# First batch of a talking-heads attention kernel: logits of 19 chunks from weighted q, without a relayout

## The chip, the cores and the metric

The kernel runs on one core of a Trainium2 chip. The metric is the time on the device in microseconds (us), as the median of three runs; lower is better. The engines are PE (TensorE, matrix products), DVE (VectorE), ACT (ScalarE), POOL (GpSimd) and SP (SyncE, which here only issues DMAs); PEld is the loading of weights into PE.

## What is computed

Attention of 12 heads whose logits are mixed over the heads before the softmax and whose weights are mixed again after it ("talking heads"), followed by a feed-forward layer with a squared relu. There are 8 batches of 448 positions, a head has 64 elements, the model 768, the hidden layer 2048.

```python
def _attn_ref(q, k, v, w_pre, w_post):
    scale = 1.0 / np.sqrt(q.shape[-1])
    scores = scale * np.matmul(q, k.transpose(0, 1, 3, 2))
    scores = np.einsum('bhij,hg->bgij', scores, w_pre)
    scores = scores - np.max(scores, axis=-1, keepdims=True)
    attn = np.exp(scores)
    attn = attn / (np.sum(attn, axis=-1, keepdims=True) + 1e-09)
    attn = np.einsum('bhij,hg->bgij', attn, w_post)
    return np.matmul(attn, v)

def _moe_ref(x, w_in, w_out):        # x: attention, heads side by side
    h = np.maximum(x @ w_in, 0.0)
    return h * h @ w_out
```

## The kernel before

A batch has 448 query rows: 384 in three blocks (r = 1, 2, 3) of 128, and a tail of 64 (r = 0). Heads go in six pairs: kt holds, for a pair, the transposed keys with one head on partitions 0 to 63 and the other on 64 to 127, qz the transposed queries of the three blocks, zt those of the tail, with zeros for the head that isn't meant.

*Scores (L660).* For each head of a block one matmul with 64 partitions and 448 columns (two heads of a pair run side by side on PE's halves), for the tail one matmul per pair. DVE or ACT copies each from PSUM to a store snat (L426, L428), whose partitions are query rows.

*Relayout (L689).* The mixing needs heads on partitions. SP issues DMAs that move 10 rows of all 12 heads (120 partitions, a chunk) from snat to a buffer sch. A batch has 45 chunks: 6 of the tail, 13 each of the blocks. Chunk 0 of a block (positions C0[1] = 6, C0[2] = 19, C0[3] = 32 of the list) takes what is left over: the last 8 rows of the block and rows of the tail or of the next block; C0[2] has its own buffer schl.

*Mixing (L784).* One matmul with the weights wmix (w_pre spread over the 10 rows, times the negative scale) makes a chunk's 120 x 448 logits. In the first batch the tail's and the first block's chunks go in threes instead: one DMA of 315 KB moves three chunks to a buffer tri (in osb or h2, which are free then), and a chunk takes three matmuls with weights wtri (L780), which are made at the start on DVE, PE and ACT (L460, L465, L472, L480, L482).

*Then, for each chunk:* minimum over a row on DVE (L789; logits have the sign turned), exponential with its sum on ACT (L792), reciprocal on DVE (L798), the second mixing's weights times that reciprocal on POOL (wq, L801), four matmuls that mix and transpose (L808), and a copy to atb by DVE or ACT. AV (L848) runs when the chunks of a block are there, its result goes to xt by ACT (L858). The feed-forward layer goes in units of 128 or 256 rows: L901 (first product), relu on ACT (L914), square on POOL (L917), L933 (second product), a copy to osb on DVE (L948), stores by SP.

*What sets the order.* A planner in the kernel itself (class Planner) simulates the engines with the costs given in `add` and writes each engine's instructions out in the order that it finds; the chip then waits where data is late. An operation has a priority, mostly its chunk's place n in the list, less some distance: a relayout has n - AHEAD, scores a little less. The feed-forward matmuls have a priority far behind all others and fill what PE has left over. Where PE would be idle early on, the planner puts in matmuls on zeros (still, L1144), which keep PE's clock up. The costs and due times near the change are these:

```python
AHEAD = 7.4
LOADS0 = [("k", 0), ("t", 0), ("t", 1), ("k", 1), ("k", 2), ("q", 0), ("q", 1), ("q", 2)]
ORDER0 = [
    *range(EARLY), *[C0[1] + 1 + c for c in TRIPLES], C0[1], *range(EARLY, C0[1]),
    C0[2], *[C0[2] + 1 + c for c in TRIPLES], C0[3], *[C0[3] + 1 + c for c in TRIPLES],
]
...
        m = m_op[n] = add(
            "PE", 570 if three else 190, n, keep(mk, f_m),
            relay[n] + [at_op.get(n - NE)] + (tri_ready[sub(b, c)] if three else [w_ready]), lat=200, bank=mk,
        )
```

At the start POOL issues the loads of k, q and the tail of q (L348, L354, L359), then, behind a small copy that waits for the tail's scores (hold, L1067), those of v and of w_in (w1, L1019). SP first issues two small DMAs that repeat w_pre and w_post over the partitions (L380, L381).

Of the kernel before, what the change touches and what calls it, by code (L numbers as in the profile page):

```python
# [11 lines left out]
F32 = mybir.dt.float32  # L12
# [30 lines left out]
AHEAD = 7.4  # L43
# [11 lines left out]
LOADS0 = [("k", 0), ("t", 0), ("t", 1), ("k", 1), ("k", 2), ("q", 0), ("q", 1), ("q", 2)]  # L55
# [3 lines left out]
def spans(odd, half):  # L59
# [8 lines left out]
TRIPLES = [4 * m + t for t in range(4) for m in range(3)]  # L68
EARLY = 6
ORDER0 = [  # L70
    *range(EARLY), *[C0[1] + 1 + c for c in TRIPLES], C0[1], *range(EARLY, C0[1]),
    C0[2], *[C0[2] + 1 + c for c in TRIPLES], C0[3], *[C0[3] + 1 + c for c in TRIPLES],
]
NTRI = 5
SOON = 0
TRI_IN = (0, 1)
W2_AT = [18, 21, 24, 27]
Q1_AT = [13, 16]
LAST_W1 = 4
TAIL0, Q0 = 19, 0.7  # L80
EARLY0 = 0
# [36 lines left out]
class Planner:  # L118
# [18 lines left out]
    def run(self):  # L137
# [39 lines left out]
        while True:  # L177
            for eng, heap in ready.items():
# [53 lines left out]
                if item is None and eng == "PE" and free and IDLE_FROM <= t < IDLE_END and (  # L232
                    clock.at(t) > 1 or clock.share(t - SPELL, t) < IDLE_LOW
# [66 lines left out]
def kernel(  # L300
# [66 lines left out]
    nc.vector.memset(qt[:, :, :], 0.0)  # L367
    for what in LOADS0:
        if what[0] == "k":
            load_kv(ks, k, 0, 4 * what[1], 4 * what[1] + 4)  # L370
        elif what[0] == "q":
            load_q(0, 4 * what[1], 4 * what[1] + 4)
        else:
            load_tail(0, what[1])
        if what == LOADS0[0]:
            masks.make_identity(nc, ident[:, :])
# [22 lines left out]
    for t_ in wmix[1:]:  # L399
# [10 lines left out]
    keep_m = sb.tile([KC, 3], F32, name="keep_m")  # L410
    nc.vector.tensor_reduce(
        out=keep_m[:, :], in_=ident[0:KC, 0:KC].rearrange("p (s m g) -> p m s g", s=CI, m=3), axis=AX.XY, op=ALU.add,
    )
    pick = [h2[0][0:KC, f, 0:KC] for f in range(6)]
    wtri_all = sb.tile([KC, 18, P], BF16, name="wtri_all")
    wtri = [[wtri_all[:, 3 * m + x, :] for x in range(3)] for m in range(6)]
    nc.gpsimd.memset(wtri_all[:, :, KC:P], 0.0)
    tri = [t_[0:KC, 0:3 * S // 2].bitcast(BF16).rearrange("k (x s) -> k x s", x=3) for t_ in osb]
    tri += [
        h2[1][0:KC, :, :].rearrange("k f c -> k (f c)")[:, 3 * S * i:3 * S * (i + 1)].rearrange("k (x s) -> k x s", x=3)  # L420
        for i in range(3)
# [32 lines left out]
    set_up = add("DVE", 6300, -100, lambda: None)  # L454

    def pick_one(tail, x):
        to = pick[3 * tail + x]
        if tail:
            for m in range(3):
                nc.vector.tensor_copy(  # L460
                    out=to[:, :].rearrange("k (s m x g) -> k m s x g", s=CI, m=3, x=2)[:, m],
                    in_=ident[0:KC, 0:KC].rearrange("k (s g y x) -> k y s x g", s=CI, g=2, y=3)[:, x],
                )
        else:
            nc.vector.tensor_copy(  # L465
                out=to[:, :].rearrange("k (s m g) -> k s m g", s=CI, m=3),
                in_=ident[0:KC, 0:KC].rearrange("k (s g x) -> k x s g", s=CI, x=3)[:, x].unsqueeze(2).to_broadcast([KC, CI, 3, 4]),
            )

    def spread(tail, slot):  # L470
        for x in range(3):
            nc.tensor.matmul(  # L472
                slot[0:KC, x * KC:(x + 1) * KC], lhsT=pick[3 * tail + x][:, :], rhs=wmix[1][:, 0:KC], start=True, stop=True,
            )

    def thin(eng, tail, m):
        src = slots["g", "tri", tail][0:KC, 0:3 * KC].rearrange("p (x k) -> p x k", x=3)
        to = wtri_all[:, 9 * tail + 3 * m:9 * tail + 3 * m + 3, 0:KC]
        if eng == "DVE":
            nc.vector.tensor_scalar(out=to, in0=src, scalar1=keep_m[:, m:m + 1], scalar2=1.0, op0=ALU.mult, op1=ALU.mult)  # L480
        else:
            nc.scalar.activation(out=to, in_=src, func=ACT.Copy, scale=keep_m[:, m:m + 1])  # L482

    tri_ready = {}
    for tail in (1, 0):
        key = ("g", "tri", tail)
        at_pri = -30 if tail else -17
        picks = [add("DVE", 250, at_pri, lambda tail=tail, x=x: pick_one(tail, x), [set_up]) for x in range(3)]
        mm = add("PE", 200, at_pri, keep(key, lambda slot, tail=tail: spread(tail, slot)), picks, lat=200, bank=key)
        thins = []  # L490
        for m in range(3):
            thins.append(add(
                {"DVE": 500, "ACT": 560}, 0, at_pri + 0.1 * m, lambda eng, tail=tail, m=m: thin(eng, tail, m), [mm],
            ))
            tri_ready.setdefault(3 * tail + m, []).append(thins[-1])
        free_ = add("FREE", 0, at_pri, lambda: None, thins, lat=0, frees=key)
# [9 lines left out]
    def used(b, piece):  # L506
        i = 2 * b + piece - NSLOT
        return [score_ops[i // 2, NJ, PIECE * (i % 2) + x] for x in range(PIECE)] if i >= 0 else []
# [34 lines left out]
    def t_tail(b, g):  # L543
        key = ("f" if b == 0 else "g", "z", b, g)
        old = [score_ops[b - 1, 0, p] for p in range(3 * g, 3 * g + 3)] if b > 0 else []
# [12 lines left out]
        pri = b * NCHUNK - (19 if b > 0 else TAIL0) + 3 * g  # L558
# [3 lines left out]
        for p in range(3 * g, 3 * g + 3):  # L562
            ready_tail[b, p] = ev

# [620 lines left out]
```

## Time and profile before

| | us |
|---|---|
| median of three runs | 589.08 (588.86 to 589.49) |
| the profiled execution | 587.99 |
| its span in the trace | 586.2 |
| PE busy | 569.0 (97%) |
| of that, matmuls on zeros (L1144), 51 | 8.9 |
| DVE / ACT / POOL busy | 486.9 / 470.5 / 326.4 |
| first mixing matmul (L780) | starts at 18.94 |
| first feed-forward matmul (L901) | starts at 54.17 |

Busy time of PE is modelled with the end of each matmul, so one that stands alone looks longer than its place in a row of them: the distance of two starts is the price. The granted clock is PE's, 1.00 being full. A group's row gives its line, engine, operation, output and inputs, count, busy us, mean ns of one, and the idle time of the engine just before, with what ended it.

The largest groups of the chunks' work:

```profile
L792 ACT ACTIVATE es<-bank,mn 120x448 bf16<-120x448 f32 x360 | 229.6, 644 | 39.2 <-DVE mn L789 34.1
L789 DVE TENSOR_REDUCE mn<-bank 120x1 f32<-120x448 f32 x360 | 210.2, 612 | 7.7 <-PE bank L780 4.5
L426 DVE CAST snat<-bank 128x448 bf16<-128x448 f32 x164 | 96.3, 614 | 4.8 <-PE bank L660 3.3
L428 ACT CAST snat<-bank 128x448 bf16<-128x448 f32 x172 | 84.9, 551 | 3.7 <-PE bank L660 2.9
L801 POOL TENSOR_SCALAR wq<-wback,rc 120x120 bf16<-120x120 f32 x360 | 130.6, 367 | 179.1 <-DVE rc L798 104.0
```

### The profile page before, as it was taken

To read this page: it belongs to the slowest core of one execution; us is meant where nothing else is said; L and a number is where in the kernel's file an instruction comes from. 1 tells how busy PE (TensorE), PEld (TensorE's weight loads), DVE (VectorE), ACT (ScalarE), POOL (GpSimd) and SP (SyncE) were. 2 spreads that over 40 slices of the span, in tenths; PEclk is the share of its full clock that TensorE was granted. 3 is DMA by queue.
4 is the path that set the end of the run, shared out by engine and by line. 5 is a ranking of instruction groups with operands and counts; after the bars stand their busy time and mean duration, and the time that the engine had idled before them with its cause. 6 is when DMAs were issued, how large, how long until landed. Compare 5 with 4: busy or idle time off the path is not lost.

```text
span 586.2 us, 17120 instructions
## 1 busy us (share of the span) xinstructions
PE 569.0 (97%) x5802; PEld 407.8 (70%) x5802; DVE 486.9 (83%) x1241; ACT 470.5 (80%) x1239; POOL 326.4 (56%) x600
## 2 busy tenths in 40 slices
PE   8798999999999999999999999999999999999996
PEld 5446866777668676767767776876767766868783
DVE  5698999998899999999898888989798898989201
ACT  4597998889888898988888878888889888788330
POOL 4537557546666538744865538744856633735340
PEclk9899999999999999999999999999999999999999
DMA  8999969964796449965797639954597547322021
GB/s 96 190 216 221 208 143 174 192 160 116 130 196 164 122 115 173 190 134 142 114 173 171 135 100 173 184 146 124 100 176 177 133 112 146 102 82 79 1 55 54
DMA packets 132086, 82.33 MB, mean 140 GB/s; under 512 B 59582, under 2 KB 126286, under 8 KB 131998
## 3 DMA queue, kind: packets, MB, share of 16 engines
q1 hardware_dynamic: 85214, 58.42, 41.1%
q0 software_dynamic: 46784, 22.81, 30.9%
q8 instruction: 45, 0.74, 0.6%
q14 instruction: 43, 0.35, 0.2%
HBM read 45.62 MB, written 11.01 MB: 97 GB/s over the span
## 4 chain that ended last, share of the span: by engine, by line
PE 85%; ACT 4%; DMA 3%; DVE 3%; POOL 2%; issue 2%; SPq 0%; DVEq 0%; POOLq 0%; ACTq 0%
PE bank L933 24%; PE bank L901 24%; PE bank L808 13%; PE bank L784 10%; PE bank L848 6%; PE bank L660 6%; ACT es L792 2%; DMA sch<-snat 1%; DVE mn L789 1%; DMA osb<-snat 1%; PE bank L780 1%; ACT snat L428 1%; ACT hr L914 1%; PE bank L522 1%; DMA qt<-in_q_dram 1%
## 5 line engine op out<-in xcount | busy, mean ns | idle before, releaser
L792 ACT ACTIVATE es<-bank,mn 120x448 bf16<-120x448 f32 x360 | 229.6, 644 | 39.2 <-DVE mn L789 34.1
L801 POOL TENSOR_SCALAR wq<-wback,rc 120x120 bf16<-120x120 f32 x360 | 130.6, 367 | 179.1 <-DVE rc L798 104.0
L789 DVE TENSOR_REDUCE mn<-bank 120x1 f32<-120x448 f32 x360 | 210.2, 612 | 7.7 <-PE bank L780 4.5
L933 PE MATMUL bank<-w,h 128*128 128x384 bf16 x896 | 174.3, 325 | 0.9 <-ACT es L792 0.5
L426 DVE CAST atb<-bank 112x480 bf16<-112x480 f32 (+3 forms) x227 | 142.5, 636 | 28.9 <-PE bank L808 26.2
L901 PE MATMUL bank<-xt,w 128*128 128x256 bf16 (+1 forms) x1632 | 164.5, 253 | 0.2
L901 PEld LDWEIGHTS <-w 128*128 128x128 bf16 x1632 | 135.7, 98 | 21.9 <-issue 2.3
L917 POOL TENSOR_TENSOR h<-hr 128x512 bf16<-128x512 f32 x112 | 116.3, 1039 | 54.2 <-ACT hr L914 51.9
L808 PEld LDWEIGHTS <-es 120*112 120x112 bf16 (+1 forms) x1440 | 116.7, 130 | 38.2 <-issue 7.6
L808 PE MATMUL bank<-wq,es 120*112 120x120 bf16 (+1 forms) x1440 | 129.1, 217 | 3.0 <-POOL wq L801 2.0
L933 PEld LDWEIGHTS <-h 128*128 128x128 bf16 x896 | 83.5, 97 | 54.9 <-issue 5.2
L784 PE MATMUL bank<-sch,wmix 120*128 120x448 bf16 x334 | 103.2, 353 | 0.3
L426 DVE CAST snat<-bank 128x448 bf16<-128x448 f32 x164 | 96.3, 614 | 4.8 <-PE bank L660 3.3
L428 ACT CAST atb<-bank 112x480 bf16<-112x480 f32 (+3 forms) x157 | 82.5, 541 | 16.3 <-PE bank L808 14.7
L914 ACT ACTIVATE hr<-bank 128x512 f32<-128x512 f32 x112 | 67.1, 599 | 30.9 <-PE bank L901 25.2
L428 ACT CAST snat<-bank 128x448 bf16<-128x448 f32 x172 | 84.9, 551 | 3.7 <-PE bank L660 2.9
L792 ACT ACTIVATION_READ_ACCUMULATOR es<-bank,mn 120x1 f32 x360 | 76.0, 211 | 0.0
L798 DVE RECIPROCAL rc<-sm 120x1 f32<-120x1 f32 x360 | 53.4, 155 | 14.2 <-ACT es L792 12.0
L948 DVE COPY osb<-bank 128x384 f32<-128x384 f32 x56 | 30.9, 551 | 31.6 <-PE bank L933 31.3
L660 PE MATMUL bank<-kt,qz 64*128 64x448 bf16 x288 | 42.5, 354 | 0.4 <-ACT atb L428 0.2
L784 PEld LDWEIGHTS <-wmix 120*128 120x128 bf16 x342 | 30.3, 98 | 16.6 <-issue 6.7
L848 PE MATMUL bank<-atb,vs 112*64 112x192 bf16 (+3 forms) x864 | 41.0, 250 | 0.4 <-ACT atb L428 0.4
(60 smaller groups left out, 261.8 us busy)
## 6 DMA issues: line engine op xcount, KB each, us to landing
sch<-snat SPq DMA_DIRECT2D x318, 105.0 KB
out_dram<-osb SPq DMA_DIRECT2D x23, 360.0 KB
vs<-in_v_dram POOLq DMA_DIRECT2D x16, 336.0 KB, 9.0
ks<-in_k_dram POOLq DMA_DIRECT2D x14, 336.0 KB, 9.9
qs<-in_q_dram POOLq DMA_DIRECT2D x14, 288.0 KB, 8.9
w<-in_moe_w_in_dram POOLq DMA_DIRECT2D x6, 512.0 KB, 20.9
w<-in_moe_w_out_dram POOLq DMA_DIRECT2D x4, 768.0 KB, 25.1
out_dram<-osb SPq DMA_DIRECT2D x8, 192.0 KB
```

Of the source, the lines that this page charges most:

```text
L426: nc.vector.tensor_copy(out=out_, in_=in_)
L428: nc.scalar.copy(out=out_, in_=in_)
L660: nc.tensor.matmul(slot[:, 0:S], lhsT=lhsT, rhs=kt[i][half, :, at_, :], start=True, stop=True)
L784: nc.tensor.matmul(slot[:, 0:S], lhsT=wm[0:rows, :], rhs=src[0:rows, :], start=True, stop=True,)
L789: nc.vector.tensor_reduce(out=mn[i][0:rows, :], in_=slots[mk][0:rows, 0:S], axis=AX.X, op=ALU.min)
L792: nc.scalar.activation(out=es[i][0:rows, 0:S], in_=slots[mk][0:rows, 0:S], func=ACT.Exp, scale=-1.0, bias=mn[i][0:rows, 0:1], accum_out=sm ...
L801: nc.gpsimd.tensor_scalar(out=wq[i][0:rows, :, 0:ns], in0=wback[0:rows, :, 0:ns], scalar1=rc[i][0:rows, 0:1], scalar2=1.0, op0=ALU.mult, o ...
L808: nc.tensor.matmul(slot[0:P_KEYS, jb * H * ns:(jb + 1) * H * ns], lhsT=es[i][0:rows, jb * P_KEYS:(jb + 1) * P_KEYS], rhs=wq[i][0:rows, :, ...
L848: nc.tensor.matmul(v_[64 * hh:64 * hh + 64, i, 0:x1 - x0], lhsT=vs[:, 2 * c2 + hh, jb, :], rhs=atb[half][:, jb, 2 * c2 + hh, x0:x1], start ...
L901: nc.tensor.matmul(slot[:, j * w:(j + 1) * w], lhsT=w1[c2][:, (f0 + j) * 128:(f0 + j + 1) * 128], rhs=xt[:, c2, a:z], start=(c2 == 0), sto ...
L917: nc.gpsimd.tensor_tensor(out=h2_[:, f0:f0 + nf, 0:w], in0=hr[gi % 2][:, :].rearrange("p (f c) -> p f c", f=nf), in1=hr[gi % 2][:, :].rear ...
L933: nc.tensor.matmul(slot[:, 0:384], lhsT=h2_[:, ft, mt * 128:(mt + 1) * 128], rhs=w2[:, ft, nt * 384:(nt + 1) * 384], start=(ft == 0), stop ...
```

## The change

In the first batch the chunks below C0[2], 19 of them, no longer go through scores, store and relayout. Mixed logits are a sum over heads of w_pre times q times k, so q is weighted first: for each chunk, DVE or POOL multiplies the chunk's 10 columns of qz (or zt) by wfan (w_pre times the negative scale, repeated over ten rows), which gives for each pair a matrix of 128 partitions by 120 columns (head g and row s). Six matmuls, one per pair, with kt as the moving operand, add up to the chunk's logits. The weighted matrices (qw) lie in four halves of the two osb buffers, so a chunk's preparation waits for the mixing four chunks before it. The order of a chunk's 120 rows is then head first, so it uses a second spread of w_post (wback_far).

Chunk C0[2] still takes rows from block 2 by DMA, but its tail rows come from weighted q too (wlast, six more matmuls). C0[1] now takes rows of its own block and the tail alone. The triples, their weights and their buffers go; block 2's and block 3's chunks come in plain order.

With it come: the tail of q by one DMA into a free buffer and one set of six transposes (first_tail), AHEAD 6.4, v's and w1's loads without the wait for hold (w1 with the priorities of the first six chunks), matmuls on zeros in every gap before 9 us, the second feed-forward product of a unit waiting, in the planner's list, for the squares that it needs first rather than for all, and wfan, zeroing and the second spread of w_post in the set-up, with three more small DMAs on SP.

```diff
-AHEAD = 7.4
+AHEAD = 6.4
-LOADS0 = [("k", 0), ("t", 0), ("t", 1), ("k", 1), ("k", 2), ("q", 0), ("q", 1), ("q", 2)]
+LOADS0 = [("k", 0), ("t", 0), ("k", 1), ("k", 2), ("q", 0), ("q", 1), ("q", 2)]
...
+NEAR_TO = C0[2]
 ORDER0 = [
-    *range(EARLY), *[C0[1] + 1 + c for c in TRIPLES], C0[1], *range(EARLY, C0[1]),
-    C0[2], *[C0[2] + 1 + c for c in TRIPLES], C0[3], *[C0[3] + 1 + c for c in TRIPLES],
+    *range(EARLY), *range(C0[1] + 1, C0[2]), C0[1], *range(EARLY, C0[1]), C0[2],
+    *range(C0[2] + 1, C0[3]), *range(C0[3], NCHUNK),
 ]
+NQW = 4
+PREP = {1: {"DVE": 450, "POOL": 1500}, 2: {"DVE": 260, "POOL": 800}}
+PREP_AT = 2
+W1_AT = [0, 1, 2, 3, 4, 5]
+W1_GATE = 0
...
-                    clock.at(t) > 1 or clock.share(t - SPELL, t) < IDLE_LOW
+                    t < 9000 or clock.at(t) > 1 or clock.share(t - SPELL, t) < IDLE_LOW
...
+    qt0 = kn[0:NS, :, :, :].rearrange("t j h d -> t (j h d)")[:, 0:DMODEL].rearrange("t (h d) -> t h d", h=H)
+    wrep = sb.tile([P, NPAIR, H], F32, name="wrep")
+    wfan = qn[:, :, :, :].rearrange("p r h d -> p (r h d)")[:, 0:NPAIR * KC].rearrange("p (c g s) -> p c g s", c=NPAIR, g=H)
+    wlast = many(2, "wlast", [P, NPAIR * 24 + P - 24], BF16)
+    for x in range(2):
+        nc.sync.dma_start(out=wrep[64 * x:64 * x + 64, :, :], in_=w_pre[x:H:2, :].unsqueeze(0).to_broadcast([D, NPAIR, H]))
+    nc.sync.dma_start(out=wpost_far[:, :], in_=w_post[:, :].unsqueeze(1).to_broadcast([H, CI, H]))
...
-            load_tail(0, what[1])
+            nc.gpsimd.dma_start(out=qt0, in_=q[0, :, TAIL:S].rearrange("h t d -> t h d"))
...
+    nc.vector.tensor_scalar(
+        out=wfan, in0=wrep[:, :, :].unsqueeze(3).to_broadcast([P, NPAIR, H, CI]),
+        scalar1=-SCALE, scalar2=1.0, op0=ALU.mult, op1=ALU.mult,
+    )
...
+    def first_tail():
...
+            for p in range(NPAIR):
+                nc.tensor.transpose(
+                    v_[:, p * NS:(p + 1) * NS], qt0[:, 2 * p:2 * p + 2, :].rearrange("t x d -> t (x d)"), ident[0:NS, 0:NS],
+                )
...
+    def is_direct(b, c):
+        return b == 0 and c < NEAR_TO
...
+        if far:
+            j = len(direct) % NQW
+            old = [m_op[direct[-NQW]]] if len(direct) >= NQW else []
...
+                def f_prep(eng, first=first, size=NPAIR // parts, x=x, s0=s0, w=w):
+                    o = 2 if w == 8 else 0
+                    src_ = x[:, 0, :, s0:s0 + w] if size < NPAIR else x[:, :, s0:s0 + w]
+                    (nc.vector if eng == "DVE" else nc.gpsimd).tensor_tensor(
+                        out=qw[j][:, first:first + size, :].rearrange("p c (g s) -> p c g s", g=H)[:, :, :, o:o + w],
+                        in0=src_.unsqueeze(2).to_broadcast([P, size, H, w]),
+                        in1=wfan[:, first:first + size, :, 0:w], op=ALU.mult,
+                    )
+
+                got.append(add(PREP[parts], 0, n - PREP_AT, f_prep, old + late + [set_up], lat=100))
+            mix_deps, mix_ns = got + [ready[0, p][0][0] for p in range(NPAIR)], 1130
+        elif b == 0 and c in C0[1:3]:
...
+            prep_op.append(add("POOL", 500, n - 6, f_last, [tail_ready], lat=100))
+            mix_deps, mix_ns = [prep_op[-1]], 1320
...
         def f_m(slot):
...
+            for p in range(NPAIR):
+                i_, at_ = slot_of(0, p)
+                n_ = KC if far else 24 if p < NPAIR - 1 else P
+                nc.tensor.matmul(
+                    slot[0:n_, 0:S], lhsT=qw[j][:, p, :] if far else wl[:, 24 * p:24 * p + n_],
+                    rhs=kt[i_][:, :, at_, :], start=far and p == 0, stop=p == NPAIR - 1,
+                )
...
-                                   [prev] + sq_op[ix] + w2_in[0:1 if ix < SOON else 4], lat=0, bank=key)
+                                   [prev] + sq_op[ix][0:4 // nf] + w2_in[0:1 if ix < SOON else 4], lat=0, bank=key)
...
+            if not is_direct(0, c):
+                relayout(0, c)
             chunk(0, c)
+            for i, at in enumerate(W1_AT):
+                if n == at:
+                    load_w1(i, n, gate(n) if W1_GATE else [])
```

In the changed kernel's instruction order POOL gets 16 preparations of 360 elements, one of 720, one of 144 and two of 144 for wlast, DVE five of 720, eight of 360 and two of 288.

## The prediction

> **What bounds the kernel now.** I read the page's head first, then busy time by stretches, then the chain that ended last, then TensorE's timeline up to the first feed-forward matmul. A change of 0.2% (1.2 us) is about what a measurement of this kernel can tell from no change.
>
> The head and two stretches of 465 and 26 us:
>
> ```profile
> span 586.2 us, 17120 instructions
> PE 569.0 (97%) x5802; PEld 407.8 (70%) x5802; DVE 486.9 (83%) x1241; ACT 470.5 (80%) x1239; POOL 326.4 (56%) x600
> 95.00:560.00 465.00, 463.30 (x4633) 335.44 (x4632) 405.81 (x1025) 390.07 (x1036) 266.06 (x494) 1.00 0.71 138
> 560.00:586.20 26.20, 21.50 (x164) 15.82 (x162) 2.79 (x5) 4.78 (x8) 8.31 (x8) 0.95 0.16 46
> ```
>
> The columns of a stretch are its length, then busy us (instructions) of PE, PEld, DVE, ACT and POOL, then granted clock, DMA share and GB/s. From 95 to 560 us PE stands still for 1.7 of 465 us, so a pass added to PE costs its full length there, and a pass is only cheap where PE has a hole. The holes lie in the first 95 us:
>
> ```profile
> 20.00:25.00 5.00, 2.21 (x10) 0.85 (x8) 2.09 (x6) 1.96 (x6) 2.02 (x4) 0.90 1.20 225
> 25.00:30.00 5.00, 4.78 (x33) 3.06 (x32) 4.22 (x10) 3.08 (x8) 1.07 (x3) 0.76 1.12 268
> 35.00:40.00 5.00, 4.54 (x36) 2.62 (x35) 4.92 (x15) 5.00 (x16) 1.46 (x4) 1.00 1.09 206
> 45.00:50.00 5.00, 3.62 (x33) 2.43 (x33) 5.00 (x13) 3.86 (x11) 4.94 (x10) 1.00 1.36 224
> 85.00:90.00 5.00, 4.29 (x77) 3.27 (x76) 4.48 (x15) 5.00 (x17) 2.79 (x7) 1.00 0.50 149
> ```
>
> At 20 to 25 us PE is less than half busy and its clock then falls to 0.76. From 30 to 50 us DVE and ACT are full instead. The chain says what opened the first hole, and the timeline where it ends:
>
> ```profile
> 15.81 7.74 DMA osb<-snat
> 18.94 1.86 PE L780 MATMUL bank<-osb,wtri_all 120*128 120x448 bf16 x9 [0.25 <-DMA osb<-snat]
> 23.59 2.10 PE L780 MATMUL bank<-osb,wtri_all 120*128 120x448 bf16 x6 [2.79 <-DMA osb<-snat]
> 36.02 0.36 PE L660 MATMUL bank<-kt,qz 64*128 64x448 bf16 x2
> 36.32 0.74 PE L780 MATMUL bank<-h,wtri_all 120*128 120x448 bf16 x3
> 36.90 0.37 PE L808 MATMUL bank<-wq,es 120*112 120x120 bf16 x4
> 37.11 0.73 PE L780 MATMUL bank<-h,wtri_all 120*128 120x448 bf16 x3
> 54.17 1.51 PE L901 MATMUL bank<-xt,w 128*128 128x128 bf16 x24
> ```
>
> A triple relayout took 7.74 us on the chain. The first mixing matmul starts at 18.94, the first feed-forward one (L901) at 54.17. From then on PE nearly always has filler of value. The distances of starts give prices: three 448-column passes take 36.90 - 36.32 = 0.58, so 0.19 us a pass; the four of L808 take 0.21, and up to 0.31 elsewhere; I use 0.25.
>
> **The change part by part.**
>
> *PE work.* Nineteen chunks mix with 6 passes, 114 in all, and chunk 19 (C0[2]) gets 6 more: 120 x 0.19 = +22.8. Gone are 54 passes of L780 and one of L784 (55 x 0.19 = -10.5), six score passes with zt and twelve half-height ones that run in pairs (12 x 0.19 = -2.3), and six spreads and half of the tail transposes (about -1, from 0.50 + 0.51 of L472's two rows). Net +9.0 us of PE work, all before the old 54 us mark.
>
> *Its start.* A direct chunk needs kt of all six pairs and, for the tails, zt. In the timeline the last k transposes start at 10.89, and the last DVE copy to kt is 12.17 + 0.38 = 12.55. I put the first mix at 12.7, 6.2 before 18.94. Of what goes before it: wfan waits for w_pre in two DMAs of 48-byte pieces, queued first on SP ahead of the old two, and makes 720 elements on DVE. Setup on DVE was done at 5.95 (5.48 + 0.47); wmix's wait for a later SP issue may put it at 7, still well ahead of the copies at 11. On POOL the tail load moves up to second place, past the second k load (issued at 2.37 before, one issue of about 0.75 later now); the third k load, at 4.75 before, does not move back. w_turn and its two wmix copies move from before the first score to beside the k transposes: 0.3 of PE and 0.5 of DVE, in time in which both wait for loads. The bounds of the first mix are 11.9 (end of the last k transposes) and 15 (setup 2.5 late, and the four preps behind it).
>
> *From first mix to first feed-forward matmul.* The changed kernel's instruction order has between them 125 full passes (23.8), 24 half-height ones (12 pairs x 0.30, from 36.02 to 36.32 in the timeline, = 3.6), 21 groups of four at L808's place (5.3), 24 q transposes (twice the 0.53 that L522 took for twelve, = 1.1) and the two AV groups (1.53 + 0.95 = 2.5). Sum 36.3. 12.7 + 36.3 = 49.0 if PE never waits. It will wait a little: the chain from the last block-1 mix to AV is max 0.61, exp 0.64, accumulate 0.21, reciprocal 0.16, wq 0.37, L808 0.37, atb 0.66, about 3.0, and 4.3 of PE work lies beside it in the order; before, the same stretch took 7.6 (43.3 to 50.86) with DVE and ACT full. I add 2.5 and get **51.5**. Two mixes (24 for 26) and one group of four fewer are done by then, 0.6 us. Gain 54.2 - 51.5 - 0.6 = **-2.1**. The bounds are -4.6 (no wait) and, by POOL's pace below, about +4.5.
>
> *DVE and ACT.* Removed: 18 snat evictions (0.614 and 0.551, about 10.5), picks and thins (0.98 + 0.47 + 1.7 + 1.6 = 4.8), three of four zt copies (1.2). Added on DVE by the order: five preps of 720 elements, eight of 360, two of 288. No row shows this form. Below: a bf16 SBUF copy, qn 279 ns for 384 and kn 322 for 512, 0.34 ns an element, so 0.39 for 720. Above: one element a cycle as in L426's 448 in 614, so 0.9. The form is bf16 in SBUF like the copies but reads two tensors; I take 0.5, 0.3 and 0.25, so 2.5 + 2.4 + 0.5 = 5.4 (4.2 to 9), plus wfan and memsets about 1.8. Net some 9 us less for two engines, 4.7 each. PE, not they, sets the pace of the direct stretch.
>
> *POOL.* It gets 16 preps of 360, one of 720, one of 144 and two wlast of 144. Two groups price them:
>
> ```profile
> L917 POOL TENSOR_TENSOR h<-hr 128x512 bf16<-128x512 f32 x112 | 116.3, 1039 | 54.2 <-ACT hr L914 51.9 <-DVE rc L798 1.8
> ...
> L405 POOL TENSOR_TENSOR wback<-wpost_rep,smask 120x120 f32<-120x120 f32 x1 | 0.4, 434 | 0.0
> ```
>
> A group gives busy us and mean ns of one. 434 ns for 120 elements and 1039 for 512 make 1.54 ns an element on 0.25, so 0.80, 1.36 and 0.47. Queued on POOL between first and last direct mix: 16 x 0.80 + 1.36 + 3 x 0.47, 18 wq at 0.367 (6.6) and a w1 issue 0.75, together 22.9. PE's work there is 114 passes, 17 groups of four, 16 half passes and the q transposes: 21.7 + 4.3 + 2.4 + 1.1 = 29.5. So preps hide with 6.6 to spare. Each wq stands behind one or two preps on POOL, and L808 and then atb wait for wq; the ring of six chunks covers that.
>
> *DMA.* Six relayouts of 315 KB, two pieces of the C0[1] one, and one tail piece of schl leave SP; SP then starts with block 2. v and w1 no longer wait for the hold copy at 14.91: their issues (1.6 + 4.3 of POOL time, one w1 apart) start near 8, behind the q loads and ahead of the first POOL prep, and end near 14, before the first wq. The six w1 loads took 15.8 to 26.9 to land and overlapped the triples. I give it nothing: no PE wait for w1 shows.
>
> *The second hole.* In 85 to 90 us PE idles 0.7 and runs 0.9 of filler while ACT is full; with 80 to 85 it is 2.2. ACT and DVE arrive with 4.7 us less behind them, and the second feed-forward product waits, in the planner's list, for four squares instead of sixteen. I take half: **-1.1** (0 to -2.2).
>
> *The rest.* AHEAD 6.4 for 7.4 issues each relayout a chunk later, in every batch; SP's moves behind it shift alike. Waits of L784's weight loads for sch are 1.9 us in the whole run. I take 0 (-0.5 to +3). The finer square waits change the order of L933 where PE is full anyway: 0. The last unit's groups (L901 to 571.10, L933 from 571.11) have no gap to close.
>
> **Sum.** The profiled execution took 587.99 (span 586.2 and 1.8 around it): 587.99 - 2.1 - 1.1 = 584.8. The median of the runs shown is 1.1 above it, so 585.9; I say **586.0**.
>
> **Rivals.**
>
> *POOL sets the pace; slower.* From 1.2 us for a prep of 360 (0.80 + 6.6/16) POOL outlasts PE in the direct stretch, every mix waits for its prep, and PE runs filler. At 1.5 us POOL needs 34.1, 4.6 more than PE, so L901 starts at 56.1, the second hole stays, and the kernel ends at 589.1 + 56.1 + 0.6 - 54.2 = 591.6. For it: a broadcast in both inputs with runs of ten elements, priced from longer runs. Against: L405 has such runs and a broadcast, and fits. SBUF — State Buffer of the Trainium skill (two separate sides) says that a VectorE operation with two SBUF inputs and a GpSimd one that reads SBUF lock each other out for the whole instruction. By that rule each of the 15 DVE preps can hold POOL for its 0.3 to 0.5 us or be held for 0.80; 15 x 0.4 = 6.0 would use up nearly all that POOL has to spare, and no run here shows yet whether it happens.
>
> *The gain is given back.* Start at 15 instead of 12.7, since the preps stand behind setup on DVE: 2.3 later, second hole half closed; 586.0 + 2.3 = 588.3, and with that hole open 589.4. For it: DVE has wfan and the w_pre DMA ahead of everything. Against: DVE idled 2.87 before L480 in that stretch.
>
> *More goes than I count.* No wait before AV and the second hole closed: 586.0 - 2.5 - 1.1 = 582.4. For it: 2 MB less relayout at a DMA share above 1. Against: ACT and DVE still evict block 2 in the same stretch.
>
> **How the numbers follow.** Forecast 0.50 (584 to 587.9), more 0.10, given back 0.14 (588 to 590.2), POOL 0.26 (above 590.2). Faster 0.50 + 0.10 = 0.60, same 0.14, slower 0.26. The range runs from 582.3 to 592.0; that leaves out under 0.05 below and some 0.12 above, where a prep costs over 1.5. The likeliest case alone has 584 to 587.9.
>
> **What would show it.** The first direct mix near 12.7; clock 1.0 from 20 to 30; prep on POOL 0.8 and on DVE 0.3 to 0.5; L901's counterpart near 51.5; PE standing less than 2 us between; nothing changed after 95 except by a shift. I am wrong if PE waits for osb (the preps) in the direct stretch, if the first mix is past 15, or if mixes after 95 wait for sch.

## The result, and the profile after

The changed kernel takes **597.37 us** (median of four runs, 595.48 to 600.81) beside 589.20 (588.86 to 589.49) for the kernel before in the same comparison: a ratio of 1.0147, 95% interval 1.0116 to 1.0178. It is 8.2 us slower. The forecast was 586.0, faster; the time lies outside the range of 582.3 to 592.0.

The profiled execution took 596.15. The head of its page, then its stretches (length, busy us of PE, PEld, DVE, ACT and POOL with instructions, granted clock, DMA share, GB/s):

```profile
span 594.3 us, 17146 instructions
PE 574.1 (97%) x5826; PEld 413.1 (69%) x5826; DVE 487.6 (82%) x1245; ACT 467.6 (79%) x1221; POOL 341.4 (57%) x614
```

```profile
10.00:15.00 5.00, 4.50 (x50) 3.30 (x52) 3.60 (x10) 0.97 (x2) 1.66 (x3) 0.50 1.35 165
...
20.00:25.00 5.00, 2.75 (x12) 1.43 (x10) 1.78 (x4) 1.84 (x5) 4.98 (x7) 0.78 1.18 210
...
35.00:40.00 5.00, 5.00 (x40) 3.60 (x39) 3.84 (x11) 4.01 (x12) 4.54 (x9) 1.00 0.16 31
...
45.00:50.00 5.00, 5.00 (x36) 2.85 (x34) 3.84 (x10) 3.38 (x10) 4.74 (x9) 1.00 1.08 140
...
85.00:90.00 5.00, 4.93 (x55) 3.09 (x52) 4.85 (x14) 3.93 (x11) 3.72 (x7) 1.00 0.18 38
100.00:110.00 10.00, 8.36 (x66) 4.66 (x64) 7.80 (x20) 7.60 (x21) 5.07 (x10) 1.00 1.22 184
180.00:190.00 10.00, 7.45 (x68) 5.29 (x68) 8.23 (x22) 7.90 (x22) 6.46 (x13) 1.00 1.21 161
95.00:560.00 465.00, 459.13 (x4639) 332.40 (x4639) 413.67 (x1049) 396.02 (x1042) 270.52 (x499) 1.00 0.70 140
560.00:594.30 34.30, 29.71 (x242) 21.45 (x236) 3.90 (x7) 6.54 (x11) 8.33 (x8) 0.98 0.17 47
```

Three things stand out. The granted clock is 0.50 in the slice before the direct mixing begins. (Below, before_sqfine shows 0.50 in that slice too, with the first 50 us of the kernel before left as they were, and its two marks come 0.4 and 0.5 us late; so the change need not be the reason.) The hole at 20 to 25 is still there, with POOL now full in it. And between 95 and 560 us PE stands for 5.9 us where it stood for 1.7: the hole at 85 to 90 closed, but others opened at 100 to 110 and 180 to 190. PE's timeline around the first mix (L798), the first wait and the first feed-forward matmul (L915):

```profile
7.95 0.58 PE L500 MATMUL bank<-ident,ks 112*64 112x112 bf16 x16 [2.03 <-DMA ks<-in_k_dram]
...
15.68 1.49 PE L798 MATMUL bank<-kt,osb 128*120 128x448 bf16 x6
...
22.61 0.40 PE L823 MATMUL bank<-wq,es 120*112 120x120 bf16 x4 [2.25 <-POOL wq L816]
...
56.80 1.40 PE L915 MATMUL bank<-xt,w 128*128 128x128 bf16 x22
```

The first mix starts 3.3 earlier than before the change, the first feed-forward matmul 2.6 later. The chain of waits (start, length, what) tells which path led to that first wait:

```profile
3.19 0.80 SPq L389
4.03 9.16 DMA wpost_rep<-in_w_post_dram
13.34 0.77 POOL wback L414
14.11 0.64 POOL wback_far L433
14.75 1.54 POOL vs L360 x2
16.29 2.56 POOL w L1036 x4
...
19.87 1.77 POOL osb L765
21.64 0.58 POOL wlast L778
22.22 0.35 POOL wq L816
```

A small load of w_post that SP issues as the fifth takes 9.16 us. wback, which needs it, stands on POOL ahead of v's and w1's issues, these ahead of POOL's first preparation of q, and that ahead of the first wq. The loads of k were late as well, as the view of DMA issues shows (KB each, median us from issue to landing), first before the change, then after it:

```profile
ks<-in_k_dram POOLq DMA_DIRECT2D x3, 224.0 KB, 4.0
```

```profile
ks<-in_k_dram POOLq DMA_DIRECT2D x3, 224.0 KB, 9.0
```

Same loads, same size, 5 us later, and yet the 16 DMA engines were less busy: their mean share in the first 10 us is 0.58, and was 0.97.

### The profile page after: what moved, and what is told of

It reads as the page before. It is cut to its first block, busy times and chain, and to the rows that moved or that the text cites. A ratio compares the mean times of both kernels' runs of the same rounds, so it can differ in the third digit from the quotient of the medians.

```text
span 594.3 us, 17146 instructions
## 1 busy us (share of the span) xinstructions
PE 574.1 (97%) x5826; PEld 413.1 (69%) x5826; DVE 487.6 (82%) x1245; ACT 467.6 (79%) x1221; POOL 341.4 (57%) x614
## 3 DMA queue, kind: packets, MB, share of 16 engines
q1 hardware_dynamic: 85172, 56.40, 38.9%
## 4 chain that ended last, share of the span: by engine, by line
PE 86%; DMA 6%; ACT 2%; POOL 2%; DVE 2%; issue 1%; SPq 1%; DVEq 0%; ACTq 0%; POOLq 0%
PE bank L947 24%; PE bank L915 23%; PE bank L823 13%; PE bank L790 10%; PE bank L862 7%; PE bank L651 6%; DMA sch<-snat 4%; PE bank L798 4%; DMA wpost_rep<-in_w_post_dram 2%; ACT es L807 1%; ACT hr L928 1%; POOL w L1036 1%; PE bank L500 1%; DVE snat L445 0%; DVE atb L445 0%
## 5 line engine op out<-in xcount | busy, mean ns | idle before, releaser
L816 POOL TENSOR_SCALAR wq<-wback,rc 120x120 bf16<-120x120 f32 (+1 forms) x341 | 124.4, 368 | 180.3 <-DVE rc L813 114.6
L915 PE MATMUL bank<-xt,w 128*128 128x256 bf16 (+1 forms) x1632 | 164.7, 253 | 0.9 <-DVE atb L445 0.5
L445 DVE CAST atb<-bank 112x480 bf16<-112x480 f32 (+3 forms) x227 | 136.4, 614 | 32.8 <-PE bank L823 29.5
L915 PEld LDWEIGHTS <-w 128*128 128x128 bf16 x1632 | 135.8, 98 | 24.4 <-issue 4.4
L823 PEld LDWEIGHTS <-es 120*112 120x112 bf16 (+1 forms) x1440 | 114.4, 130 | 40.3 <-issue 11.2
L823 PE MATMUL bank<-wq,es 120*112 120x120 bf16 (+1 forms) x1440 | 126.8, 217 | 7.8 <-POOL wq L816 3.5
L790 PE MATMUL bank<-sch,wmix 120*128 120x448 bf16 x333 | 104.9, 354 | 1.8 <-DMA sch<-snat 1.6
L447 ACT CAST atb<-bank 112x480 bf16<-112x480 f32 (+2 forms) x157 | 83.8, 544 | 22.6 <-PE bank L823 19.9
L445 DVE CAST snat<-bank 128x448 bf16<-128x448 f32 x163 | 94.5, 611 | 6.3 <-PE bank L651 2.8
L447 ACT CAST snat<-bank 128x448 bf16<-128x448 f32 x155 | 76.6, 545 | 3.4 <-PE bank L651 3.2
L790 PEld LDWEIGHTS <-wmix 120*128 120x128 bf16 (+1 forms) x341 | 29.9, 97 | 18.0 <-issue 8.8
L862 PEld LDWEIGHTS <-vs 112*64 112x64 bf16 x864 | 36.5, 110 | 4.2 <-issue 3.7
```

What stands on the lines that cost most here:

```text
L445: nc.vector.tensor_copy(out=out_, in_=in_)
L447: nc.scalar.copy(out=out_, in_=in_)
L790: nc.tensor.matmul(slot[:, 0:S], lhsT=wm[0:rows, :], rhs=src[0:rows, :], start=True, stop=mix_ns == 190,)
L816: nc.gpsimd.tensor_scalar(out=wq[i][0:rows, :, 0:ns], in0=back[0:rows, :, 0:ns], scalar1=rc[i][0:rows, 0:1], scalar2=1.0, op0=ALU.mult, op ...
L823: nc.tensor.matmul(slot[0:P_KEYS, jb * H * ns:(jb + 1) * H * ns], lhsT=es[i][0:rows, jb * P_KEYS:(jb + 1) * P_KEYS], rhs=wq[i][0:rows, :, ...
L862: nc.tensor.matmul(v_[64 * hh:64 * hh + 64, i, 0:x1 - x0], lhsT=vs[:, 2 * c2 + hh, jb, :], rhs=atb[half][:, jb, 2 * c2 + hh, x0:x1], start ...
```

## The experiments

PE's standing time in the table is 465 us less its busy time in 95 to 560 us of the run's profile; the ratio has its 95% interval. The two marks and the standing time come from one profiled execution each. Two of one kernel (wide_hold and wide_hold74) differ by 1.0 at the first feed-forward matmul and by 0.2 in standing. The profiled execution is the fastest of ten for wide and the slowest for wide_half and wide_ahead74, so it need not stand for the median.

| run | ratio to the kernel before | first mix | first feed-forward | PE stands in 95 to 560 |
|---|---|---|---|---|
| before | 1 | 18.94 | 54.17 | 1.7 |
| the changed kernel | 1.0147 (1.0116 to 1.0178) | 15.68 | 56.80 | 5.9 |
| before_pieces | 1.0105 (1.0083 to 1.0126) | 24.67 | 60.24 | 1.5 |
| wide | 1.0057 (1.0039 to 1.0076) | 12.84 | 49.84 | 5.8 |
| ahead74 | 1.0150 (1.0128 to 1.0173) | 15.72 | 58.65 | 6.1 |
| half_passes | 1.0105 (1.0070 to 1.0140) | 15.48 | 54.18 | 6.6 |
| wide_sqall | 1.0116 (1.0098 to 1.0134) | 13.26 | 50.29 | 8.8 |
| before_sqfine | 1.0023 (1.0004 to 1.0041) | 19.38 | 54.64 | 4.2 |
| wide_ahead74 | 1.0048 (1.0027 to 1.0069) | 13.33 | 55.48 | 7.0 |
| wide_tails | 1.0022 (1.0004 to 1.0040) | 13.53 | 56.40 | 2.4 |
| wide_half | 0.9998 (0.9978 to 1.0018) | 13.36 | 50.29 | 8.0 |
| wide_half2 | 0.9931 (0.9905 to 0.9957) | 13.12 | 45.96 | 4.9 |
| wide_prephalf | 1.0078 (1.0050 to 1.0106) | 13.49 | 51.51 | 6.9 |
| wide_hold | 1.0017 (1.0001 to 1.0034) | 13.25 | 57.45 | 6.7 |
| wide_hold74, the same kernel | 1.0029 (1.0014 to 1.0045) | 13.23 | 56.43 | 6.5 |
| wide_split | 1.0126 (1.0086 to 1.0167) | 12.89 | 50.80 | 7.5 |
| before_ahead64 | 1.0154 (1.0134 to 1.0175) | 21.14 | 59.87 | 5.7 |

### The small loads: wide and before_pieces

```diff
-    wrep = sb.tile([P, NPAIR, H], F32, name="wrep")
+    wrep = sb.tile([P, NPAIR, 2, H], F32, name="wrep")
...
-    for x in range(2):
-        nc.sync.dma_start(out=wrep[64 * x:64 * x + 64, :, :], in_=w_pre[x:H:2, :].unsqueeze(0).to_broadcast([D, NPAIR, H]))
+    nc.sync.dma_start(
+        out=wrep[:, :, :, :].rearrange("p c x g -> p (c x g)"),
+        in_=w_pre[:, :].rearrange("h g -> (h g)").unsqueeze(0).to_broadcast([P, H * H]),
+    )
```

wide repeats w_pre by 128 pieces of 576 bytes instead of 768 of 48.

> Edit: in the changed kernel, w_pre is repeated for the weighting by 128 pieces of 576 bytes instead of 768 of 48 bytes (one DVE instruction more). Theory A, that the many small pieces on SP hold up the first loads of k and the tail and so the first direct mix (15.7 us, with PE at half clock to 16 and again from 23 to 26): the first k transposes come near 6 instead of 7.9, the first direct mix near 13, and the time falls by 3 to 5 us from the changed kernel's 597. Rival B, that the start does not matter because DVE and ACT set the pace of the first batches anyway: under 1 us.

It took 592.28, some 5.1 us less than the changed kernel, as theory A said. Its first mix and first feed-forward matmul:

```profile
12.84 1.35 PE L801 MATMUL bank<-kt,osb 128*120 128x448 bf16 x6
...
49.84 1.51 PE L918 MATMUL bank<-xt,w 128*128 128x128 bf16 x24
```

before_pieces does the reverse. The kernel before gets the change's three extra small loads ahead of everything on SP and uses none of them:

```diff
+    wrep = sb.tile([P, NPAIR, H], F32, name="wrep")
+    wpost_far = sb.tile([KC, H], F32, name="wpost_far")
+    for x in range(2):
+        nc.sync.dma_start(out=wrep[64 * x:64 * x + 64, :, :], in_=w_pre[x:H:2, :].unsqueeze(0).to_broadcast([D, NPAIR, H]))
+    nc.sync.dma_start(out=wpost_far[:, :], in_=w_post[:, :].unsqueeze(1).to_broadcast([H, CI, H]))
```

> Edit: the kernel before, with the changed kernel's three extra small loads (w_pre twice, w_post once, 888 pieces of 48 bytes) issued first on SP, their data not used. Theory A: the first k transposes move from 5.3 to about 8 us and the first mixing matmul from 18.9 to about 21.5; the time rises by 2 to 3 us from 589. Rival B: the loads of k are late in the changed kernel for another reason (the order of the loads on POOL), and nothing moves by more than 0.5 us.

It took 594.90, 6.1 us more, twice what theory A had said, and both marks moved by about the same: 5.7 at the first mix, 6.1 at the first feed-forward matmul. k's loads landed 7.7 us after their issue instead of 4.0. PE's standing after 95 us stayed (1.5). So 888 pieces of 48 bytes, issued first, cost the kernel before 6 us, and a late start of that kernel is carried to the end whole. In the changed kernel, widening 768 of them gave back 5.1. There k's loads landed 6.6 us after their issue, still later than the 4.0; the tail's load now stands ahead of the second of them, and how much of the rest is due to that was not tried.

### Passes, preparations and the pace of the direct stretch

half_passes leaves out three of a direct chunk's six passes, and with them the heads of three pairs; wide_half does the same to the wide kernel:

```diff
-            for p in range(NPAIR):
+            for p in range(NPAIR // 2 if far else 0, NPAIR):
...
-                    rhs=kt[i_][:, :, at_, :], start=far and p == 0, stop=p == NPAIR - 1,
+                    rhs=kt[i_][:, :, at_, :], start=far and p == NPAIR // 2, stop=p == NPAIR - 1,
```

> Edit: the changed kernel, each of the 19 direct chunks with three of its six mixing matmuls (heads of three pairs are left out of those chunks' logits; order and everything else as in the changed kernel). It takes away 57 passes of 0.19 us, 10.8 us of PE work. Theory D, that the added passes cost their full length because PE has no other hole that they fill: the time falls by 7 to 11 us from 597, to below the kernel before. Rival, that preparation on POOL and DVE, or the late start, sets the pace of the direct stretch: it falls by less than 3 us.

> The kernel with the wide load, with three of the six passes of each direct chunk (57 passes of 0.19 us fewer, 10.8 us of TensorE work); the heads of three pairs are left out of the first 19 chunks. The order of instructions is the same. In the wide kernel TensorE is 10.00 of 10 busy from 20 to 40 us, so there each pass is on the path. Theory G (work removed there is carried to the end): first feed-forward matmul near 43 and 582 to 584. Theory K (from block 2 on attention goes at a pace that other engines set, an earlier start only brings feed-forward work forward, and this work is missing when attention waits at 140 to 250 us): first feed-forward matmul at 43 to 47 and yet 588 to 591.5.

10.8 us of PE work gone brought the changed kernel only 2.2 us (595.17), as the rival had said; PE waits 8.1 us for wq between 13 and 55 us there. The wide kernel fell to 589.63, some 3 us, but its first feed-forward matmul did not move at all (49.84 to 50.29), which neither theory had expected. PE's waits between 13 and 50 us in wide_half (us in total, times, longest) say why:

```profile
PE bank L826 <- POOL wq L819: 5.6, 12, 0.9
```

So wide_half2 also leaves out the preparations of the pairs that it does not use, and wide_prephalf has all passes with half of the preparations:

```diff
                def f_prep(eng, first=first, size=NPAIR // parts, x=x, s0=s0, w=w):
+                    if size < NPAIR and first == 0:
+                        return
+                    h_ = size if size < NPAIR else PIECE
+                    first = PIECE
...
-                    lhsT=qw[j][:, p, :] if far else wl[:, 24 * p:24 * p + n_],
+                    lhsT=qw[j][:, PIECE + p % PIECE, :] if far else wl[:, 24 * p:24 * p + n_],
```

(the last pair of lines in wide_prephalf alone)

> The kernel with the wide load and three of the six passes of each direct chunk, and now without the weighting of q for the three pairs left out: 13 of the 26 preps of block 1 are gone (about 9 on GpSimd at 0.86 and 4 on VectorE), those of the tails are half as long. The heads of three pairs are left out of the first 19 chunks; the order of what is left is the same. With half of the passes alone, GpSimd was full from 15 to 45 us (5.00 of 5 in most slices), TensorE waited twelve times for wq, and the first feed-forward matmul stayed at 50.3. Theory L (GpSimd's queue sets the pace of the direct stretch beside TensorE): first feed-forward matmul at 43 to 46, and hardly a wait for wq. If it stays near 50, VectorE and ScalarE set that pace. The time then tells whether an earlier start is carried to the end: 581 to 585 if it is (theory G), 587 to 590 if from block 2 on another pace holds (theory K).

> The kernel with the wide load and all its passes, but with q weighted for three pairs only: the six passes of a direct chunk read three weighted pairs twice, so the scores of the first 19 chunks are wrong sums, with the same TensorE work. GpSimd and VectorE are relieved as in the run before, TensorE is not. If GpSimd alone set the pace of the direct stretch: first feed-forward matmul near 46, and 587 to 588. If TensorE and GpSimd are level there (10.00 of 10 busy both, in the wide kernel): first feed-forward matmul at 48.5 to 50, and 590 to 592.5.

Relieving both moved the first feed-forward matmul from 50.29 to 45.96 and took 585.35. Relieving POOL alone left it at 51.51 and took 594.36, 2 us more than wide and more than the 592.5 expected; why it is slower was not settled. The stretch of 25 to 30 us in wide, wide_half and wide_prephalf, in this order, shows both limits (PE busy is the first number behind the length, POOL busy the fifth):

```profile
25.00:30.00 5.00, 5.00 (x38) 3.31 (x36) 3.93 (x11) 4.42 (x13) 4.79 (x9) 1.00 1.12 212
```

```profile
25.00:30.00 5.00, 3.61 (x28) 2.15 (x28) 4.68 (x13) 4.77 (x14) 5.00 (x8) 1.00 1.12 211
```

```profile
25.00:30.00 5.00, 5.00 (x38) 3.18 (x37) 4.29 (x11) 4.46 (x11) 2.65 (x5) 1.00 1.12 211
```

In wide PE is full (it stands 0.6 of the 37 us from 13 to 50) and POOL is close behind, so they are nearly level: with less work for PE, POOL is full, and with less work for POOL, PE still is. With both relieved, in wide_half2, DVE and ACT come next: 4.73 and 4.89 of the same 5 us. From wide_half to wide_half2 the first feed-forward matmul came 4.3 earlier and the time fell by 0.67%, 3.9 us. That fits a gain carried to the end, but the standing after 95 us fell as well (8.0 to 4.9), so it is not shown by this pair.

### The order of instructions

Two edits of the change only shift instructions. ahead74 and wide_ahead74 put AHEAD back to 7.4; before_ahead64 gives 6.4 to the kernel before:

```diff
-AHEAD = 7.4
+AHEAD = 6.4
```

> Edit: the changed kernel with AHEAD back at 7.4. Theory C, that relayouts issued a chunk later cause the waits for sch and the idle PE at 102 to 106 and 180 to 200 us: idle of PE after 95 us falls from 5.9 to about 2 us, the time by 2 to 4 us from 597. Rival: those holes come from chunks that are late already, and the time stays within 1 us.

> The kernel with the wide load and AHEAD 7.4 instead of 6.4; nothing else. Theory H (the relayouts of blocks after the first two come a chunk late, now that the direct stretch ends sooner; the two waits for sch at 90 to 100 us are its mark): 590 to 591, and those waits gone. Theories F and G: within 0.7 of the kernel with the wide load, 592.3.

> The kernel before with AHEAD 6.4 instead of 7.4, an edit that only moves instructions. Theory M: 590 to 593, with TensorE standing 3 to 6 us in 95 to 560 instead of 1.7, while the first 50 us stay as they were. If the order after 95 us does not matter: 588.5 to 589.5, and 1.5 to 2.5 us of standing.

In the changed kernel it makes no difference (597.48), although the waits for relayouts that theory C names do go: after 95 us no mix waits for sch any more (1.6 us before the edit), and the weight loads' waits for it fall from 3.3 to 1.1, yet PE stands 6.1 us. In the wide one it makes at most a little (591.40 for 592.28, intervals overlapping). In the kernel before it costs 9.7 us, more than the whole change and far more than any theory had said. Half of that comes early, against the expectation: the second group of triples waits 3.30 for its relayout, and the first feed-forward matmul comes 5.7 later. (In that profile the granted clock is lower as well, 0.60 at 10 to 15 us and 0.66 at 20 to 25 where the kernel before has 1.00 and 0.90, so not all of the 5.7 need be the order.) The rest is standing after 95 us:

```profile
95.00:560.00 465.00, 459.28 (x4651) 332.12 (x4653) 406.90 (x1034) 401.91 (x1065) 267.69 (x492) 1.00 0.71 140
```

The 5.7 and 4.0 more of standing are 9.7 of the 11.9 by which the span of this profile is longer (598.1 and 586.2). The finer waits for squares were undone in the wide kernel and done alone in the kernel before:

```diff
-                                   [prev] + sq_op[ix] + w2_in[0:1 if ix < SOON else 4], lat=0, bank=key)
+                                   [prev] + sq_op[ix][0:4 // nf] + w2_in[0:1 if ix < SOON else 4], lat=0, bank=key)
...
-                        prev = add("PE", 652, FILL, lambda key=key, mms=mms: mms(slots[key]), [prev, w2_in[f0 // 4]], lat=0)
+                        prev = add("PE", 652, FILL, lambda key=key, mms=mms: mms(slots[key]), [prev, w2_in[f0 // 4]] + sq_op[ix][0:(f0 + 4) // nf], lat=0)
```

> The kernel with the wide load, and its second products wait for all squares again, as before the change; nothing else. Theory F (the finer square waits let the second products be issued earlier; they use up feed-forward work that later stands as filler, so TensorE has holes between 90 and 190 us): 588 to 589.5, the first second product near 87 instead of 81, and TensorE busy over 98.5 of the 100 us from 100 to 200 instead of 96.9. Theory G (the order of the second products does not matter; the 9 us of added passes are the rest): 592 to 593, holes as they were.

> The kernel before with the finer square waits alone; nothing else. Theory F: 591 to 593, with the first second product several us earlier and holes between 90 and 190 us that the kernel before does not have. Theory G: 588.5 to 589.5, no change.

Undoing them costs 3.7 us instead of bringing 3: one score then waits 3.7 us for a copy to snat, and PE stands 8.8 us for 5.8. Done alone in the kernel before they cost 0.2%. Theory F falls: the finer waits help the wide kernel.

wide_tails has `NEAR_TO = C0[1]`: 72 passes fewer, and block 1 by relayout again. wide_hold makes the first feed-forward matmul wait for the 25th chunk. wide_split cuts unit (640, 896) into (640, 768) and (768, 896), with AV of batch 1's second half cut likewise.

```diff
+    ac_op[HOLD_TO].next.append(h_op[0, 0][0])
+    h_op[0, 0][0].left += 1
```

> The kernel with the wide load, with only the six chunks of the tails direct; block 1 goes through scores, evictions and relayouts again. 72 passes of 0.19 fewer and 13 single mixes and six pairs of half-height scores more: 13.7 - 2.5 - 1.8 = 9.4 us less work on TensorE; 24 snat evictions more on ScalarE and VectorE than the wide kernel has. Theory G (the added passes cost their length, all that is left over 589 comes from them): 584 to 587. Theory I (what is gained in the first 50 us is lost again in holes between 50 and 200 us, since feed-forward work is brought forward and attention's own chain through ScalarE and VectorE sets the pace there): 588 to 591, with TensorE standing 3 us or more in 100 to 200.

> The kernel with the wide load, with the first feed-forward matmul held until the 25th chunk's copy is done; nothing else. It then starts near 57 instead of 49.8, so that the work brought forward stays for later. Theory K: 590 to 592.5, no slower than the wide kernel (592.3), and the holes at 140 to 190 us smaller. Theory G: the 4 us or more for which TensorE then stands between 50 and 57 are added, 594 to 597.

wide_hold74 is a second run of wide_hold (AHEAD stays 6.4, whatever the label says).

> The held kernel a second time, on the chip of this call, beside the others: theory M (the rest of the loss is TensorE standing after 95 us in an order of instructions that does not fit the real times; any edit that only moves instructions shifts it by 1 to 4 us): 589 to 592, and TensorE's standing time in 95 to 560 between 3 and 8 us.

> The kernel with the wide load, with the last feed-forward unit of the first two batches cut into two of 128 columns, the first of which may start 13 chunks (some 18 us) earlier. Theory K (at 160 to 190 us there is no feed-forward work left that may run): the holes at 170 to 190 close (1.8 us and the drop of the clock), and one opens later, near 200 to 250, where both halves are used up; 589 to 592. If the holes at 170 to 190 stay although this work may run, K falls: they are then waits in TensorE's order that the supply of work doesn't touch.

wide_tails took 589.27: 9.4 us less PE work brought 2 to 3. wide_hold took 590.90 and again 591.29, although its feed-forward work starts 7 us later than wide's: when the filler starts does not show in the time. So where the order differs, an early first feed-forward matmul is no measure of how far a kernel is. But theory K, that filler brought forward is what is missing later, falls with wide_split (596.43): the hole at 170 to 180 grew (7.57 us busy, 9.24 in wide), with more of a second product behind the waiting mix, of which sixteen matmuls had already run:

```profile
177.64 0.90 PE L793 MATMUL bank<-sch,wmix 120*128 120x448 bf16 x2 [2.43 <-DVE snat L448]
178.34 2.12 PE L950 MATMUL bank<-w,h 128*128 128x384 bf16 x6
```

In the trace PE starts the second product only behind the late mix, as the written order has it; the supply of work did not fill the wait. All of PE's waits between 95 and 560 us that the view lists, in wide and then before:

```profile
PE bank L826 <- DVE snat L448: 1.2, 1, 1.2
PE bank L826 <- POOL wq L819: 1.2, 3, 0.5
PE bank L793 <- DMA sch<-snat: 1.1, 2, 0.6
PE bank L826 <- ACT es L810: 0.7, 1, 0.7
PE bank L918 <- DVE atb L448: 0.5, 1, 0.5
PE bank L793 <- ACT es L810: 0.3, 1, 0.3
PE bank L918 <- ACT hr L931: 0.2, 1, 0.2
```

```profile
PE bank L933 <- ACT es L792: 0.5, 1, 0.5
PE bank L808 <- ACT es L792: 0.4, 2, 0.2
PE bank L933 <- DVE osb L948: 0.2, 1, 0.2
```

No single engine is late: in wide DVE, POOL, ACT and the relayouts' DMA share the waits, with 1.1 to 1.7 us each. In the two profiles the wide kernel's start is 4.3 earlier, its standing 4.1 longer, and its mean clock in 100 to 200 us is 0.98, which is about 2 us: a sum of 1.8 for the 2.2 between the profiled executions (590.17 and 587.99). Over the whole span PE stands 17.2 us in the kernel before and 17.6 in wide: before 95 us it went from 10.9 to 7.2, and after that it came back. Why this order meets the engines so much worse than the one before was not settled.

## Why the prediction failed, by its own steps

Two steps make up most of the miss. The DMA term, "I give it nothing", left out what w_pre's small pieces do to the other loads: 5.1 us, of the 11.4 by which the forecast missed. And "the rest", put at 0, is PE's standing after 95 us: 4.2 us more in the changed kernel's profile, 4.1 more in wide's. What else is missing stays open.

- **PE work: the sum of 36.3 held.** In wide, where the pieces do not disturb, first mix to first feed-forward matmul takes 37.0 us. The net of +9.0 has no such check: PE's busy time without the matmuls on zeros is 5.1 us longer in wide than before (565.2 and 560.1), but busy time is not a price.
- **Its start, 12.7: wrong, and this is the step that cost most.** "Wfan waits for w_pre in two DMAs of 48-byte pieces" was looked at only for when DVE's setup would be ready, and "DMA" was given nothing. But the pieces delay the other loads of the start: k landed after 9.0 instead of 4.0, the first k transposes came at 7.95, the first mix at 15.68. With the pieces widened it starts at 12.84, as forecast, and the kernel is 5.1 us faster.
- **v's and w1's issues: wrong by the same cause.** They were to run from 8 to 14, ahead of the first wq. They ran from 14.69 to 20, behind a wback that waited for w_post, and PE waited 2.25 for that wq. In wide they ran from 9.27 to 14.43.
- **First feed-forward matmul, 51.5: it came at 56.80.** 3.0 of the 5.3 too much are the late start; the rest is put down to the wait for wq and the clock of 0.78 and 0.88 from 20 to 30 us. In wide it came at 49.84, better than forecast, since the 2.5 of waits that were added did not come. The upper bound given for this step, about +4.5, does not follow from its own working: POOL's pace gives 56.1 + 0.6 - 54.2 = 2.5.
- **POOL, 6.6 to spare: mis-sized.** Prices held (826 ns for a preparation of 360, 0.80 said; 387 for wq, 367 said; only that of 720 took 1.77 for 1.36). What was left out are the issues of the next batch's q, k and tail loads, 4.7 us (36.7 to 42.4 in wide), which stand in POOL's queue ahead of the last direct chunks' wq. 22.9 + 4.7 leaves 1.9 below PE's 29.5, and the runs show the two nearly level. The rival "POOL sets the pace" had the side, slower, but by luck: its price did not come, and in wide PE is the full one.
- **DVE's preparations** of 360 took 0.33 to 0.41, and 0.83 once. The estimate of 6.0 us for a lock between DVE and POOL did not come, but the lock is not refuted: a DVE preparation that starts beside a POOL one ends 0.2 us after it, in wide as in the long case. In wide it mostly starts when POOL's is nearly over, so little is lost:

```profile
26.89 0.82 POOL L768 TENSOR_TENSOR osb<-qz,qn 128x360 bf16<-128x360 bf16 x1
27.53 0.38 DVE L768 TENSOR_TENSOR osb<-qz,qn 128x360 bf16<-128x360 bf16 x1
```

In the changed kernel the one of 0.83 ran from 21.02 to 21.85, beside POOL's longest, from 19.87 to 21.64. The rule of the Trainium skill in SBUF — State Buffer (two separate sides), that a VectorE operation with two SBUF inputs and a GpSimd one that reads SBUF lock each other out, fits these times; no run here was made to test it.
- **The second hole: right, in place and size.** PE stands 0.1 us from 80 to 95 us, 1.3 before, for the 1.1 forecast. It was no gain, since as much opened elsewhere.
- **"The rest", 0, with +3 as the worst: wrong.** AHEAD and the finer waits were each judged by the instructions that they name. The kernel before stands 1.7 us after 95 us (1.5 with the small loads added), while every kernel of the table with another order stands 2.4 to 8.8. "Nothing changed after 95 except by a shift" failed: 5.9 for 1.7, and that is the larger part of why wide, with a start 4.3 earlier, is still 0.57% slower than before. That the order alone does this is shown for the kernel before (before_ahead64); for wide the added passes and the order were not separated.
- **The signs of being wrong.** Two of the three came: the first mix lay past 15, and mixes after 95 us waited for sch. The longest such wait is

```profile
104.67 0.36 PE L790 MATMUL bank<-sch,wmix 120*128 120x448 bf16 x1 [1.44 <-DMA sch<-snat]
```

and ahead74, which removes these waits, shows that they are not what costs the time.

## What to carry to other kernels

Count a DMA by its pieces, not its bytes, and look at what is queued beside it: here some 43 KB in 48-byte pieces at the start delayed the loads that the kernel waits for. When work moves from one engine to another in a stretch, add up every instruction that the receiving engine's queue holds in that stretch, DMA issues of later stages among them. And where a planner writes a fixed order for a PE that is 99% busy, a change to the order has a price of its own: measure it by an edit that moves instructions and no work before giving it zero.

## What the runs showed of the hardware

888 broadcast pieces of 48 bytes from DRAM cost 6.1 us at the start of the kernel before (6.9 ns each), while 128 pieces of 576 bytes in place of 768 of 48 gave back 5.1 in the changed one. How the pieces hold up loads of another queue is not shown; the DMA engines' mean share in the first 10 us was lower with them (0.58 for 0.97).

PE's granted clock dropped beside some waits and not beside others. In the changed kernel it is 0.78 in the slice of the 2.25 us wait and 0.88 in the next, in the kernel before 0.90 and 0.76. But in ahead74 and before_sqfine PE is busy 2.38 and 2.27 of the same 5 us, and the clock is 1.00 in both slices. What decides it these runs do not show.
